# Two chunks' first products drawn forward, two sums of x moved to accumulating DMAs, and another order of the first loads, in a gated FNet and SwiGLU kernel

## The chip, the cores and the metric

The kernel runs on one core of one Trainium2 chip. The metric is the device time of one execution in microseconds. Three runs of the kernel before took 710.97, 711.2 and 711.49 us; their median is 711.2.

## The reference

Two branches work on the same x of 2048 tokens by 512 features. Branch A is a Fourier mixing: the real part of a discrete Fourier transform over features and tokens, written as matrix products. Branch B is a SwiGLU feed-forward network with 1376 hidden units. A sigmoid of a weighted sum over x mixes the two.

```python
def reference(A_x, A_dft_seq_re, A_dft_seq_im, A_dft_hid_re, A_dft_hid_im,
              B_x, B_w1, B_w3, B_w2, gate_w):
    x = A_x
    g = _sigmoid((x * gate_w).sum(-1, keepdims=True))
    # branch A
    a_ = x @ dft_hid_re.T ; b_ = x @ dft_hid_im.T
    a = dft_seq_re @ a_ - dft_seq_im @ b_
    # branch B
    b = (_silu(x @ w1) * (x @ w3)) @ w2
    return g * a + (1 - g) * b
```

The lines between are shortened here to the products they make; x is in float32, as are all operands.

## The kernel before

**Precision.** Each float32 operand is split in two: a high half, which ScalarE writes by copying to float32r (`high`, L108), and a low half, which VectorE writes by subtracting the high half from the operand (`low`, L111). `mm3` (L117) then makes one product out of three matmuls of 128x128 by 128x512: high by high, high by low, low by high, all summed in one PSUM bank.

**The gate and up products.** The hidden units are taken in chunks of 128. For one chunk, w1 and w3 together with the two halves of the features make four blocks A11, A12 (w1) and A21, A22 (w3), each stored as 128x256; they lie in this order beside one another, except that A22 comes before A21, in the input `w13`, and `load_w` brings a chunk (or columns `lo` to `hi` of its four blocks) to a tile `ws`. x is cut likewise into B11, B12, B21, B22 for each of two groups of 1024 tokens; `load_xo` brings one block, 128x1024 or 512 KB, to a tile `xs`. A chunk and a group make an item. Most items use a scheme of seven block products instead of eight (`gate_up`). It needs sums of the blocks: of x the sums T1 = B12 - B11, T2 = B22 - T1, T3 = B22 - B12 and T4 = B21 - T2 (`SUMS`, made by `sum_xo` on VectorE, L207), each split again (`split_xo`) into the tile `xo`; of the weights four sums (`sums_wb`, L248 to L251) that go to a tile `wb`. The blocks A11, A12 and A22 are split to a tile `wa` by `prep_wa`.

**Item 0** is done plainly, with eight block products (`plain`), because no sums exist yet at the start. It is a generator: the code asks for its next piece with `next(step)` after it has prepared the operands of that piece. Its four results are C00, C10, C01 and C11. In the order of the pieces: A11 B11 into C00; A21 B11 into C10; then A12 B21 and A22 B21 complete them; then the same with B12 and B22 for C01 and C11.

**Items 1, 2, 3 ...** begin with `first1` (A11 B11 into a bank X, evicted by ScalarE to the tile s1, L285), `first2` (A12 B21 into a bank Y, added to s1 by VectorE, L293) and `gate1` (Silu of s1 on ScalarE). `gate_up(n)` then makes five further products: into X with T2, T1 (further on with B22), into Z with T3 and T4, and calls `first1` and `first2` of item n + 3 between them. The first Z product of item 1 reads T3 and the second reads T4.

**Order.** Up to the loop over `gate_up`, the instructions of each engine are put in order by the framework's scheduler, by its own costs, from the code's order and the data they need. From `manual_schedule` on they stand as written. Each engine works through its instructions in that order and waits at each for what it needs. The SP queue issues loads, the POOL queue issues stores of h (`store_h`, to `hsp`) and of wb (to `wbsp`). Before the first operands are there, TensorE runs 11 matmuls on a zero tile (L398).

**Buffers.** The four raw x blocks live in four 128x1024 places (`F4`); T2 overwrites B11's place, T3 B12's and T4 B21's, and T1 has a place of its own. The second group's blocks take the same four places, so their loads wait until the splits of T2, T3 and T4 are done. Chunk w shares its place with chunk w + 4.

**After this.** The rest of the kernel is the down projection and the Fourier products (L119 as P in the profile), which the change does not touch.

Of the kernel before, what the change touches and what calls it, by code (L numbers as in the profile page):

```python
# [9 lines left out]
AF = mybir.ActivationFunctionType  # L10
ALU = mybir.AluOpType
# [21 lines left out]
def fnet_swiglu_gate_kernel(  # L33
# [20 lines left out]
    nc = tc.nc  # L54
# [25 lines left out]
    def bank(k, name):  # L80
        return psum.tile([P, 512], F32, tag=f"ps{k}", name=name)
# [14 lines left out]
    def wide(name):  # L96
        return take(F4, [P, 1024], F32, name)
# [9 lines left out]
    def high(hi, src):  # L107
        nc.scalar.activation(hi, src, AF.Copy)  # L108

    def low(hi, lo, src):  # L110
        nc.vector.tensor_sub(lo, src, hi.bitcast(F32))  # L111

    def split(hi, lo, src):
        high(hi, src)
        low(hi, lo, src)

    def mm3(ps, ah, al, bh, bl, first, last, chain=False):  # L117
        for n, (u, v) in enumerate(((ah, bh), (ah, bl), (al, bh))):
            nc.tensor.matmul(ps, u, v, start=first and n == 0, stop=last and n == 2,  # L119
                             skip_group_check=chain)  # L120

# [67 lines left out]
    XO, ST = {}, {}  # L189
    XRAW = ("B12", "B11", "B21", "B22")  # L190
# [4 lines left out]
    def load_xo(g, k):  # L195

        if g not in XO:
            XO[g] = (xo1 if g else xo0).tile([P, 2, 7, 2, 512], F32R, tag="xo", name=f"xo{g}")
        ST[g, k] = wide(f"xs{g}_{k}")
        nc.sync.dma_start(ST[g, k], xt[g, XRAW.index(k)])  # L200

    OPS = ("B11", "B21", "B22", "T1", "T2", "T3", "T4")
    SUMS = {"T1": ("B12", "B11"), "T2": ("B22", "T1"), "T3": ("B22", "B12"), "T4": ("B21", "T2")}

    def sum_xo(g, k, t):
        ST[g, k] = t
        nc.vector.tensor_sub(t, *(ST[g, v] for v in SUMS[k]))  # L207

    def xo_parts(g, k):
        o = XO[g][:, :, OPS.index(k)]  # L210
        return flat_x(o[:, 0]), flat_x(o[:, 1]), ST[g, k]

    def split_xo(g, k):
        split(*xo_parts(g, k))
# [6 lines left out]
    def load_w(w, lo=0, hi=4):  # L221
        if lo == 0:
            WS[w] = f4_a.tile([P, 4, 256], F32, tag=f"f4_{4 + w % (LOOK + 1)}", name=f"ws{w}")
        nc.sync.dma_start(WS[w][:, lo:hi].rearrange("p a n -> p (a n)"),  # L224
                          w13[SETS[w], :, lo * 256 : hi * 256])
# [7 lines left out]
    def wa_parts(w, lo, hi):  # L233
        return (*(flat(WA[w][:, h, lo:hi]) for h in range(2)), flat(WS[w][:, lo:hi]))

    def prep_wa(w, lo=0, hi=3):

        if lo == 0:
            WA[w] = wap.tile([P, 2, 3, 256], F32R, tag="wa", name=f"wa{w}")
        split(*wa_parts(w, lo, hi))  # L240
# [24 lines left out]
    def prep_wb(w):  # L265
        sums_wb(w)
        high_wb(w)
        low_wb(w)

    def prod(ps, n, wi, xi, start, chain=False):  # L270
        w = WSET[n]
        w, wi = (WA[w], wi) if wi < 3 else (WB[w], wi - 3)
        x = XO[ITEMS[n][1]]
        for q in range(2):
            sl = slice(q * P, (q + 1) * P)
            mm3(ps, w[:, 0, wi, sl], w[:, 1, wi, sl], x[:, 0, xi, q, :], x[:, 1, xi, q, :],
                start and q == 0, q == 1, chain)
# [3 lines left out]
    def first1(n):  # L281
        x = bank(n % 4, f"X{n}")
        prod(x, n, 0, 0, True)
        s1 = s1p.tile([P, 512], F32, tag="s1", name=f"s1_{n}")
        nc.scalar.activation(s1, x, AF.Copy)  # L285
        G[n] = (x, s1)

    def first2(n):

        y = bank(4 + n % 2, f"Y{n}")  # L290
        prod(y, n, 1, 1, True)
        s1 = G[n][1]
        nc.vector.tensor_add(s1, s1, y)  # L293
        put_score(n, 0, s1)

    def gate1(n):
        nc.scalar.activation(G[n][1], G[n][1], AF.Silu)
# [19 lines left out]
    def store_h(n, k, h):  # L317

        c, g = ITEMS[n]
        j = min(c % (NP2 - 1) if c < NC - 1 else NP2 - 1, NP2 - 1)  # L320
        b = 2 * (NP2 - 1 <= c < NC - 1)
        nc.gpsimd.dma_start(hsp[g, b + k, j // 2, :, j % 2 * 512 : (j % 2 + 1) * 512], h)  # L322
# [5 lines left out]
    def run(work, n):  # L328
        for f in work.get(n, ()):
            f()  # L330

    def gate_up(n):
# [56 lines left out]
        store_h(n, 1, g1)  # L389
        run(at_end, n)  # L390

    load_w(0, 0, 1)
    load_xo(0, "B11")
    warm = s1p.tile([P, 1024], mybir.dt.bfloat16, tag="s1", name="warm")[:, :512]
    nc.vector.memset(warm, 0.0)
    wps = bank(7, "wps")
# [4 lines left out]
    def plain(b12, a21):  # L401

        c = {}

        def half(i, j, w, x, start):
            if start:
                c[i, j] = bank((0, 4, 6, 7)[2 * i + j], f"C{i}{j}")
            for r in range(2):
                sl = slice(r * P, (r + 1) * P)
                mm3(c[i, j], w(0, sl), w(1, sl), x(r, 0), x(r, 1), start and r == 0,  # L410
                    not start and r == 1)

        def wa(k):
            return lambda h, sl: WA[0][:, h, k, sl]

        def xb(k):
            return lambda q, h: XO[0][:, h, k, q, :]

        w21 = lambda h, sl: a21[:, h, sl]
        x12 = lambda q, h: b12[:, h, q * 512 : (q + 1) * 512]  # L420
        s1 = s1p.tile([P, 512], F32, tag="s1", name="s1_0")
        g1 = u4p.tile([P, 512], F32, tag="u4", name="g1_0")
        h = hp.tile([P, 1024], F32, tag="h", name="h0")
        yield half(0, 0, wa(0), xb(0), True)
        yield half(1, 0, w21, xb(0), True)
        half(0, 0, wa(1), xb(1), False)
        nc.scalar.activation(s1, c[0, 0], AF.Silu)
        yield half(1, 0, wa(2), xb(1), False)
        nc.vector.tensor_mul(h[:, :512], s1, c[1, 0])
        store_h(0, 0, h[:, :512])  # L430
        half(0, 1, wa(0), x12, True)
        yield half(1, 1, w21, x12, True)
        half(0, 1, wa(1), xb(2), False)
        nc.scalar.activation(g1, c[0, 1], AF.Silu)
        half(1, 1, wa(2), xb(2), False)
        nc.vector.tensor_mul(h[:, 512:], g1, c[1, 1])
        yield store_h(0, 1, h[:, 512:])

    load_w(0, 1, 4)
    load_xo(0, "B21")  # L440
    load_xo(0, "B12")
    load_w(1)
    load_xo(0, "B22")
    load_w(2)
    load_w(3)

    zt = parts("b12"), parts("a21")
# [3 lines left out]
    for q in range(2):  # L451
        split(XO[0][:, 0, 0, q], XO[0][:, 1, 0, q], ST[0, "B11"][:, q * 512 : (q + 1) * 512])
    next(step)
    split(a21[:, 0], a21[:, 1], WS[0][:, 3])
    next(step)
    prep_wa(0, 1, 3)
    split_xo(0, "B21")
    next(step)
# [4 lines left out]
    free(*zt)  # L463
    WS.pop(0)
    load_w(4)
    prep_wa(1)
    first1(1)
    first2(1)
    gate1(1)
    sum_xo(0, "T1", hp.tile([P, 1024], F32, tag="h", name="t1"))  # L470
    sum_xo(0, "T2", ST[0, "B11"])
    prep_wa(2)
    first1(2)
    first2(2)
    gate1(2)
    split_xo(0, "T2")
    prep_wb(1)
    sum_xo(0, "T3", ST[0, "B12"])
    split_xo(0, "T3")
    prep_wa(3)  # L480
    first1(3)
# [1 line left out]
    gate1(3)  # L483
    split_xo(0, "T1")
    prep_wa(4)
    sum_xo(0, "T4", ST[0, "B21"])
    split_xo(0, "T4")
    free(*(ST[0, b] for b in ("B11", "B21", "B12", "B22")))

# [84 lines left out]
    n = NI - 1 - LOOK  # L574
# [248 lines left out]
    def step(m):  # L823
# [19 lines left out]
        for r in range(2):  # L843
            sl = slice(r * P, (r + 1) * P)
            for n, zn in steps:
                for i in range(ni):
                    w = ws[2 * n + i]
                    b = slice(i * 512, (i + 1) * 512)
                    mm3(ps[r], w[:, 0, f, sl], w[:, 1, f, sl], zn[:, 0, b], zn[:, 1, b],
                        own and n == 0 and i == 0, n == NQ[blk] - 1 and i == ni - 1, not own)  # L850
# [57 lines left out]
    for i, (src, sp, p) in enumerate(late):  # L908
        blk, b = 1 + i // 2, i % 2
        n = (17, 24)[b]  # L910
# [84 lines left out]
```

## Time and profile before

| | us |
|---|---|
| median of three runs | 711.2 |
| the profiled execution, its own time | 710.88 |
| the span of its trace | 709.1 |
| TensorE busy | 703.9 |
| VectorE busy | 604.6 |
| ScalarE busy | 369.6 |

The profile was taken in one execution. Its time of 710.88 us contains the span of 709.1 us, from the first to the last recorded instruction, and what lies around it. The granted TensorE clock is full through the span. Times within the trace are counted from the span's start. In a row of the timeline stand the start, the duration, the engine, the line of the kernel, the operation with its tiles (out<-in), the shapes and the number of instructions merged in the row; in brackets stands how long the engine was idle before it and what released it. PE is TensorE's matmul, PEld its weight load, DVE VectorE, ACT ScalarE, POOL GpSimd, SPq the queue of SyncE. Numbers behind tile names are left out, so `xo` stands for any operand of x, `wa` for any chunk's split blocks.

### The profile page before, as it was taken

How to read it: one execution, taken by the hardware profiler on the slowest of the kernel's cores; microseconds unless marked ns; L12 is line 12 of the kernel's file. 1: busy time of each engine (PE TensorE's matmuls, PEld its weight loads, DVE VectorE, ACT ScalarE, POOL GpSimd, SP SyncE). 2: the span in 40 equal slices, each digit the busy share in tenths (PEclk: the TensorE clock that was granted, in tenths of full speed). 3: DMA queues.
4: the chain of work that ended last, by engine and by line, in shares of the span. 5: the costliest groups of instructions: out<-in, count | busy, mean ns of one | idle time of the engine just before them, and what ended most of it. 6: DMA issues, size and time to landing. Idle time of an engine off the chain costs nothing.

```text
span 709.1 us, 8589 instructions
## 1 busy us (share of the span) xinstructions
PE 703.9 (99%) x3089; PEld 579.1 (82%) x3089; DVE 604.6 (85%) x733; ACT 369.6 (52%) x478; POOL 64.0 (9%) x118
## 2 busy tenths in 40 slices
PE   9999999999999999999999999999999999999997
PEld 6888888888888888888888888888888888888886
DVE  6979988787679999887999599969997896898985
ACT  6665555655446754454554553544455455455451
POOL 0011111121110000000110001100110000000000
PEclk9999999999999999999999999999999999999999
DMA  7575546589997556712596238814999971773932
GB/s 281 196 295 215 211 188 253 186 313 359 413 412 271 220 207 232 288 60 89 175 358 254 90 122 322 342 48 190 382 419 416 354 270 58 296 285 135 323 119 89
DMA packets 45403, 172.54 MB, mean 243 GB/s; under 512 B 5296, under 2 KB 5424, under 8 KB 41520
## 3 DMA queue, kind: packets, MB, share of 16 engines
q1 hardware_dynamic: 32464, 118.50, 45.2%
q0 software_dynamic: 12608, 52.97, 18.9%
q8 instruction: 24, 0.39, 0.2%
q10 hardware_dynamic: 288, 0.52, 0.2%
q14 instruction: 19, 0.16, 0.1%
HBM read 114.82 MB, written 57.16 MB: 243 GB/s over the span
## 4 chain that ended last, share of the span: by engine, by line
PE 99%; DMA 1%; DVE 0%; ACT 0%; SPq 0%; issue 0%
PE P L119 69%; PE X L119 16%; PE Z L119 8%; PE Y L119 4%; PE C L119 2%; DMA xs_B<-xt 1%; DVE xo L111 0%; DVE zc L788 0%; ACT xo L108 0%; SPq L224 0%
## 5 line engine op out<-in xcount | busy, mean ns | idle before, releaser
L119 PE MATMUL P<-zo,a 128*128 128x512 f32 x1344 | 305.5, 390 | 0.0
L119 PEld LDWEIGHTS P<-zo,a 128*128 128x128 f32 x1344 | 252.1, 188 | 53.2 <-DVE zo L111 1.2
L108 ACT ACTIVATE zo<-B 128x1024 fp32r<-128x1024 f32 (+1 forms) x182 | 189.3, 1045 | 184.5 <-PE P L119 93.2
L111 DVE TENSOR_TENSOR zo<-B,zo 128x1024 fp32r<-128x1024 f32 (+1 forms) x182 | 217.9, 1204 | 48.2 <-ACT zo L108 47.4
L119 PE MATMUL P<-zo,H 128*128 128x512 f32 x468 | 106.2, 389 | 0.0
L119 PEld LDWEIGHTS P<-zo,H 128*128 128x128 f32 x468 | 87.9, 188 | 18.2
L645 DVE TENSOR_TENSOR B<-B,B 128x1024 f32<-128x1024 f32 (+1 forms) x78 | 93.0, 1192 | 0.1
L119 PE MATMUL X<-xo,wb 128*128 128x512 f32 x378 | 92.7, 390 | 0.0
L119 PEld LDWEIGHTS X<-xo,wb 128*128 128x128 f32 x378 | 71.0, 188 | 14.7
L119 PE MATMUL P<-zo,Y 128*128 128x512 f32 x336 | 76.3, 390 | 0.0
L119 PEld LDWEIGHTS P<-zo,Y 128*128 128x128 f32 x336 | 63.1, 188 | 13.1
L322 POOL DMA_DIRECT2D hsp<-h x42 | 23.0, 547 | 126.5 <-DVE h L373 75.6
L119 PE MATMUL X<-xo,wa 128*128 128x512 f32 x126 | 32.3, 390 | 0.0
L119 PE MATMUL Z<-xo,wa 128*128 128x512 f32 x126 | 32.3, 391 | 0.0
L119 PE MATMUL Y<-xo,wa 128*128 128x512 f32 x126 | 32.1, 390 | 0.0
L119 PE MATMUL Z<-xo,wb 128*128 128x512 f32 x126 | 32.1, 390 | 0.0
L648 DVE TENSOR_TENSOR B<-B,B 128x1024 f32<-128x1024 f32 x26 | 31.7, 1219 | 0.0
L863 ACT ACTIVATE zu<-P 128x512 f32<-128x512 f32 x32 | 19.1, 598 | 20.4 <-PE P L119 20.3
L367 DVE TENSOR_TENSOR u<-u,X 128x512 f32<-128x512 f32 x21 | 14.4, 687 | 17.7 <-PE X L119 15.5
L119 PEld LDWEIGHTS Z<-xo,wa 128*128 128x128 f32 x126 | 23.6, 188 | 5.3 <-DVE xo L111 0.4
L119 PEld LDWEIGHTS Y<-xo,wa 128*128 128x128 f32 x126 | 23.7, 188 | 4.9
L119 PEld LDWEIGHTS X<-xo,wa 128*128 128x128 f32 x126 | 23.7, 188 | 4.9
(134 smaller groups left out, 551.3 us busy)
## 6 DMA issues: line engine op xcount, KB each, us to landing
B<-cc SPq DMA_DIRECT2D x64, 512.0 KB, 6.1
hsp<-h POOLq DMA_DIRECT2D x42, 256.0 KB, 3.6
B<-hsp SPq DMA_DIRECT2D x20, 512.0 KB, 9.9
wbsp<-wb POOLq DMA_DIRECT2D x8, 1024.0 KB, 4.3
wb<-wbsp SPq DMA_DIRECT2D x8, 1024.0 KB, 7.8
B<-zsp SPq DMA_DIRECT2D x16, 512.0 KB, 8.4
H<-w2sp SPq DMA_DIRECT2D x6, 1024.0 KB, 9.0
ws<-w SPq DMA_DIRECT2D x11, 512.0 KB, 6.1
```

Source lines behind the costliest of these rows:

```text
L108: nc.scalar.activation(hi, src, AF.Copy)
L111: nc.vector.tensor_sub(lo, src, hi.bitcast(F32))
L119: nc.tensor.matmul(ps, u, v, start=first and n == 0, stop=last and n == 2, skip_group_check=chain)
L322: nc.gpsimd.dma_start(hsp[g, b + k, j // 2, :, j % 2 * 512 : (j % 2 + 1) * 512], h)
L367: nc.vector.tensor_add(u4, u4, x)
L645: nc.vector.tensor_add(t, t, RAW[blk, b, q][:, :n])
L648: nc.vector.tensor_sub(t, RAW[blk, "B12", q], t)
L863: nc.scalar.activation(U[name][:, r], ps[r], AF.Copy)
```

## The change

1. The first load issued is now B11 of x, then A11 of chunk 0. A11 of chunk 1 and of chunk 2 (128x256 each) are loaded by themselves, ahead of the rest of their chunk; A11 of chunk 1 also comes ahead of the rest of chunk 0.
2. A11 of chunks 1 and 2 are split by themselves, and `first1(1)` and `first1(2)` are called between the pieces of item 0: after A11 B11 of item 0 and after A21 B11. In the code `first2` and `gate1` of both items stay where they were.
3. In C00's products the three terms come in another order: high by high, low weights by high x, high weights by low x (`low_last`).
4. T3 and T4 are no longer made by VectorE. `minus_xo` negates the subtrahend (B12, then T2) in its own place on ScalarE and then issues, on the POOL queue, a DMA that adds the first operand (B22, then B21) from the input `xt` in device memory onto the negated tile. T4 lies therefore in the place of T2, which was B11's. T1 and T2 are sums on VectorE as before.

```diff
-    def mm3(ps, ah, al, bh, bl, first, last, chain=False):
-        for n, (u, v) in enumerate(((ah, bh), (ah, bl), (al, bh))):
+    def mm3(ps, ah, al, bh, bl, first, last, chain=False, low_last=False):
+        terms = ((ah, bh), (al, bh), (ah, bl)) if low_last else ((ah, bh), (ah, bl), (al, bh))
+        for n, (u, v) in enumerate(terms):
...
+    def minus_xo(g, k, t):
+        b, c = SUMS[k]
+        ST[g, k] = t
+        nc.scalar.activation(t, t, AF.Copy, scale=-1.0)
+        nc.gpsimd.dma_start(t, xt[g, XRAW.index(b)], accum_op=ALU.add)
...
+    load_xo(0, "B11")
     load_w(0, 0, 1)
-    load_xo(0, "B11")
...
                 mm3(c[i, j], w(0, sl), w(1, sl), x(r, 0), x(r, 1), start and r == 0,
-                    not start and r == 1)
+                    not start and r == 1, low_last=i == j == 0)
...
+    load_w(1, 0, 1)
     load_w(0, 1, 4)
+    load_w(2, 0, 1)
     load_xo(0, "B21")
     load_xo(0, "B12")
-    load_w(1)
+    load_w(1, 1, 4)
     load_xo(0, "B22")
-    load_w(2)
+    load_w(2, 1, 4)
     load_w(3)
...
     next(step)
+    prep_wa(1, 0, 1)
+    first1(1)
     split(a21[:, 0], a21[:, 1], WS[0][:, 3])
     next(step)
+    prep_wa(2, 0, 1)
+    first1(2)
     prep_wa(0, 1, 3)
     split_xo(0, "B21")
...
-    prep_wa(1)
-    first1(1)
+    prep_wa(1, 1, 3)
     first2(1)
     gate1(1)
     sum_xo(0, "T1", hp.tile([P, 1024], F32, tag="h", name="t1"))
     sum_xo(0, "T2", ST[0, "B11"])
-    prep_wa(2)
-    first1(2)
+    prep_wa(2, 1, 3)
     first2(2)
     gate1(2)
+    minus_xo(0, "T3", ST[0, "B12"])
     split_xo(0, "T2")
     prep_wb(1)
-    sum_xo(0, "T3", ST[0, "B12"])
+    minus_xo(0, "T4", ST[0, "T2"])
     split_xo(0, "T3")
...
     prep_wa(4)
-    sum_xo(0, "T4", ST[0, "B21"])
     split_xo(0, "T4")
```

## The prediction

> **What bounds the kernel now.** I read the page first: the busy shares and the chain that ended last.
>
> ```profile
> span 709.1 us, 8589 instructions
> ...
> PE 703.9 (99%) x3089; PEld 579.1 (82%) x3089; DVE 604.6 (85%) x733; ACT 369.6 (52%) x478; POOL 64.0 (9%) x118
> ...
> PE 99%; DMA 1%; DVE 0%; ACT 0%; SPq 0%; issue 0%
> ```
>
> TensorE sets the time almost alone: 99% of the span and of the chain. The change leaves the number of matmuls as it is, so it can only win time in which TensorE waits, and any new wait of TensorE lengthens the kernel one to one. The timeline of the first 20 us and of 19 to 45 us shows where it waits.
>
> ```profile
> 0.74 0.39 SPq L224 DMA_DIRECT2D ws<-w  x1
> 1.19 0.42 SPq L200 DMA_DIRECT2D xs_B<-xt  x1
> ...
> 3.21 0.42 ACT L108 ACTIVATE wa<-ws 128x256 fp32r<-128x256 f32 x1 [0.96 <-DMA ws<-w]
> ...
> 4.94 1.15 ACT L108 ACTIVATE xo<-xs_B 128x512 fp32r<-128x512 f32 x2 [1.31 <-DMA xs_B<-xt]
> ...
> 5.60 1.29 DVE L111 TENSOR_TENSOR xo<-xs_B,xo 128x512 fp32r<-128x512 f32 x2 [1.51 <-ACT xo L108]
> ...
> 5.62 0.50 PE L119 MATMUL C<-xo,wa 128*128 128x512 f32 x1
> ...
> 6.35 1.43 PE L119 MATMUL C<-xo,wa 128*128 128x512 f32 x5 [0.22 <-DVE xo L111]
> ...
> 7.19 1.06 ACT L108 ACTIVATE xo<-xs_B 128x1024 fp32r<-128x1024 f32 x1 [0.27 <-DMA xs_B<-xt]
> ...
> 8.46 1.06 ACT L108 ACTIVATE b<-xs_B 128x1024 fp32r<-128x1024 f32 x1 [0.21 <-DMA xs_B<-xt]
> ...
> 8.98 3.15 PE L119 MATMUL C<-xo,wa 128*128 128x512 f32 x12
> ...
> 9.57 2.14 PEld L119 LDWEIGHTS C<-xo,wa 128*128 128x128 f32 x10 [0.40 <-DVE xo L111]
> 9.74 0.84 ACT L108 ACTIVATE wa<-ws 128x768 fp32r<-128x768 f32 x1 [0.22 <-DMA ws<-w]
> ```
>
> ```profile
> 20.29 1.36 PE X L119 x6
> ```
>
> ```profile
> 31.00 1.83 PE L119 MATMUL Z<-xo,wa 128*128 128x512 f32 x6
> ...
> 31.40 0.99 PEld L119 LDWEIGHTS Z<-xo,wa 128*128 128x128 f32 x5 [0.43 <-DVE xo L111]
> ```
>
> Six matmuls take 1.36 us on the chain (0.227 each), and a recorded group of n ends 0.39 us after its last start. So twelve should show 11 x 0.227 + 0.39 = 2.89 us; the group at 8.98 shows 3.15, a wait of about 0.25. Six should show 1.53; the group at 31.00 shows 1.83, a wait of 0.30. The third wait is the second matmul: the first stands at 5.62, the next at 6.35. Together with that half microsecond some 1.05 us can be won, 0.15% of the time. After that no wait of note stands in the chain.
>
> The same rows show what the waits hang on: all three end with VectorE's low half of a split of x. VectorE is full there:
>
> ```profile
> 15.00:20.00 5.00, 5.00 (x24) 4.15 (x23) 5.00 (x9) 3.89 (x7) 0.41 (x1) 1.00 0.04 14
> 20.00:25.00 5.00, 5.00 (x24) 4.15 (x23) 5.00 (x6) 3.53 (x5) 0.68 (x2) 1.00 0.66 234
> 25.00:30.00 5.00, 5.00 (x24) 4.14 (x23) 4.92 (x7) 2.88 (x6) 0.00 (x0) 1.00 0.40 156
> ```
>
> In these windows by 5 us the third busy column is VectorE: 5.00, 5.00 and 4.92 of 5. So whatever leaves VectorE or comes to it before 31 us counts.
>
> **How I walk through the changed program.** I take each engine's instructions in the changed program's order and start each when its engine is free and its inputs are there, with these durations and overlaps:
>
> ```profile
> L111 DVE TENSOR_TENSOR xo<-xs_B,xo 128x1024 fp32r<-128x1024 f32 x7 | 8.6, 1222 | 0.6 <-ACT xo L108 0.6
> L111 DVE TENSOR_TENSOR wa<-ws,wa 128x768 fp32r<-128x768 f32 x7 | 6.7, 952 | 0.0
> L108 ACT ACTIVATE xo<-xs_B 128x1024 fp32r<-128x1024 f32 x7 | 7.4, 1058 | 0.8 <-DVE xs_B L207 0.5 <-DMA xs_B<-xt 0.3
> L285 ACT ACTIVATE s<-X 128x512 f32<-128x512 f32 x7 | 4.2, 594 | 3.6 <-PE X L119 3.6
> L293 DVE TENSOR_TENSOR s<-s,Y 128x512 f32<-128x512 f32 x6 | 4.1, 680 | 0.0
> L250 DVE TENSOR_TENSOR wu<-ws 128x256 f32<-128x256 f32 x5 | 2.1, 419 | 0.0
> ```
>
> ```profile
> 21.60 1.22 DVE L111 TENSOR_TENSOR wb<-wu,wb 128x1024 fp32r<-128x1024 f32 x1
> ...
> 22.74 1.22 DVE L111 TENSOR_TENSOR xo<-xs_B,xo 128x1024 fp32r<-128x1024 f32 x1
> ```
>
> Back to back, two VectorE instructions of 1.22 start 1.14 apart, so 0.08 of each is overlap; ScalarE overlaps by 0.10 (two halves of 0.62 take 1.15 above). From the end of VectorE's low half to the matmul it releases there are 0.05 (5.60 + 0.69 = 6.29, matmul at 6.35); where TensorE had been idle, the weight load is no longer hidden, another 0.11.
>
> **Part 1, the first x block first.** The queue moves 512 KB in 1.27 us (the seen landings 7.19, 8.46, 9.74). B11 was seen at 4.94, with 128 KB ahead of it. If the issue time decides it lands 0.45 earlier (1.19 - 0.74), at 4.49; if the bytes decide, 128 KB or 0.32 earlier, at 4.62. I take 4.54, between them. ScalarE's first half then ends at 5.16, VectorE's low half runs 5.19 to 5.88. But wa's high half now comes after B11 (its bytes land by 4.94, ScalarE 5.06 to 5.47), and its low half after that of B11: 5.80 to 6.21. The new order of the three terms asks for exactly this one at the second matmul. It stands at 6.26 instead of 6.35 (6.37 with its weight load): -0.09, with the two landings -0.14 and -0.01.
>
> **Part 2, A11 B11 of chunks 1 and 2 in between.** Twelve matmuls move forward, 2.72 us of cover before B21 is needed. B21 now lands behind 1,792 KB instead of 1,536 KB: 7.19 + 0.64 = 7.8. ScalarE does not take it then, because the eviction of X1 stands ahead of it and waits for X1's last matmul (6.37 + 10 x 0.227 + 0.39 = 9.03): eviction to 9.67, B21's high half to 10.63, VectorE's low half 10.66 to 11.88. The matmul that reads it is the 27th, at 6.37 + 25 x 0.227 = 12.05. Just in time: the 0.25 at 8.98 goes, -0.25. The split of wa into two pieces for two chunks costs VectorE two more instructions, two issues more on SP (0.45 each, ahead of B21) that the full queue covers. B12, B22 and the rests of the two chunks land at most 0.64 later than before, and ScalarE comes to each of them over a microsecond after that.
>
> **Part 3, VectorE's chain after it.** VectorE idles from 8.4 to 10.66 and is then busy without a gap worth counting up to the low half of T3. In the changed order that stretch holds nine of 128x1024, one of 128x768, six of 128x512 and four of 128x256: 9 x 1.22 + 0.95 + 6 x 0.685 + 4 x 0.42 = 17.7, less 19 overlaps of 0.084 is 16.1, plus about 0.3 of short waits: it ends at 27.07. T1's low half stands ahead of T3's in this order, which it did not before. The matmul that reads T3's low half is the 92nd, due at 6.37 + 90 x 0.227 = 26.80; it can start at 27.07 + 0.16 = 27.23. A new wait: +0.43. I leave 0.2 on either side for the short waits.
>
> **Part 4, T3 and T4 by accumulating DMA.** Two VectorE sums of 1.22 go; two negations on ScalarE (1.06 each by the 128x1024 row) and two 512 KB DMAs on POOL come. For T4: VectorE ends T2's low half at 22.39, ScalarE negates 22.75 to 23.81, POOL issues at 24.12 (0.31 after its releaser, the first two rows below). T4's low half is wanted by the 110th matmul, 27.23 + 18 x 0.227 = 31.31. Back from it: low half ended by 31.15, begun by 29.9, high half begun by 28.8. So the DMA may take 4.7 us. T3's, issued at 19.02, may take 5.7, for ScalarE is at T3 only at 24.75, after the Silu of chunk 2.
>
> ```profile
> 12.24 0.69 DVE L429 TENSOR_TENSOR h<-s,C 128x512 f32<-128x512 f32 x1 [0.25 <-PE C L119]
> ...
> 13.25 0.69 POOL L322 DMA_DIRECT2D hsp<-h  x1 [12.80 <-DVE h L429]
> ```
>
> ```profile
> hsp<-h POOLq DMA_DIRECT2D x42, 256.0 KB, 3.6
> ...
> wbsp<-wb POOLq DMA_DIRECT2D x8, 1024.0 KB, 4.3
> ```
>
> ```profile
> DMA to landing us min/median/max: 5.0/5.0/5.0
> ```
>
> ```profile
> DMA to landing us min/median/max: 8.6/8.6/8.6
> ```
>
> ```profile
> 28.63 4.03 SPq L200 DMA_DIRECT2D xs_B<-xt  x4
> ...
> 32.76 6.83 SPq L224 DMA_DIRECT2D ws<-w  x2
> ```
>
> No accumulating DMA stands in the trace. From POOL, 256 KB take 3.6 us from issue to landing and 1024 KB 4.3 in the median. The two rows after that are single stores of 1024 KB: the one issued at 23.1, almost alone on the queues, with 5.0, and the one at 34.7, beside the loads in the last rows, with 8.6. An accumulate reads 512 KB from memory and 512 KB from the tile, so it lies nearest the 1024 KB rows. I take 4.5, between 4.3 and 5.0: T4 lands at 28.6 and TensorE doesn't wait. The bounds are 3.6 and 8.6. With T4 in time, the 0.30 that stood at 31.00 goes: -0.30; at 5.0 it would stay. SP's loads of the second x half, at 28.63 before, now wait for T4's split (about 30.9), and the chunk load behind them leaves at 32.8 as before, so nothing follows there. On POOL's queue T4 stands behind the second store of h, which its multiply frees at 21.1, and ahead of the store of wb at 25.0, which nobody reads soon.
>
> The Trainium skill, Collectives: The Full Stack, section "The bandwidth ceiling: the fold count and why AG ≠ RS ≠ AR", says that a DMA that adds has two sources to read on one ring and so gets half of the copy's rate. By that rule, an estimate: 2 x 1.27 = 2.54 us of transfer where a copy has 1.27; the sum stays as it is so long as the rest of the DMA stays under 2.1 us. No trace here shows an accumulate yet.
>
> **Sum.** -0.09 - 0.25 + 0.43 - 0.30 = -0.21 us. The profiled execution took 710.88 with its span of 709.1, so 710.7 for it. The median of the runs is 711.2, 0.3 above: 711.0.
>
> **Rivals.**
> 1. The accumulate is late, and the kernel is slower. Place: T4's high half on ScalarE, and everything queued behind it there (Silu of chunk 3, evictions of Z1 and X4). From 4.7 us on, each microsecond of the DMA is one of TensorE's. At 8.6: 711.0 + 3.9 = 714.9. For it: the 8.6, the 5.0 of the store that stood in the same place, and that nothing here shows what an addition costs. Against it: the 8.6 came beside six loads, and in 24 to 29 us the changed program has none under way. It exceeds 0.2% (1.42 us, about what a measurement of this kernel can tell from no change) from about 6.3 us.
> 2. A little late, 4.7 to 6.3 us: 711.0 to 712.6, about 711.8 at 5.5.
> 3. T3's wait is not there, because VectorE has slack in it that I have not seen: -0.64, 710.6. Against it: the sum of part 3 is of durations that scatter by a few ns.
> 4. The change moves but doesn't win: small loads of 128 KB hold B11's followers up, the landing is byte-bound (-0.01), and B21's low half, just in time by 0.01, comes 0.1 late: -0.03, 711.2.
>
> **Chances.** Forecast 0.40, with its own range 710.6 to 711.4; rival 1 0.38 (an operation without a price, and the smallest margin of the walk hangs on it); rival 2 0.11; rival 3 0.05; rival 4 0.06. Above 0.2% stands rival 1: slower 0.38. Faster by 1.42 us is more than all the waits together; it keeps 0.03 out of rival 3 for something unseen. The rest, 0.59, is within 0.2%. The range leaves out 0.03 below 710.4 and, of rival 1, what lies over 715.0.
>
> **What would show it.** The second matmul at 6.26; no idle before the 25th to 30th matmul (the first group of A12 B21); a wait of about 0.43 at the first Z, released by VectorE's xo; issue to landing of the two accumulates near 4.5, and no wait at T4's product near 31.3. Wrong if the accumulates take over 4.7, which shows as TensorE waiting for ScalarE or VectorE at the Z group that reads wa, or if TensorE waits before 20 us.

## The result and the profile after

| | before | after |
|---|---|---|
| median of six runs, us | 711.27 (710.97 to 712.11) | 715.58 (713.59 to 715.71) |
| ratio, with its 95% interval | | 1.0055 (1.0045 to 1.0066) |
| the profiled execution, us | 710.88 | 715.66 |

The changed kernel is slower by 4.3 us. Its page begins with these rows: the span, the busy times, and the chain that ended last.

```profile
span 713.9 us, 8604 instructions
...
PE 706.0 (99%) x3089; PEld 579.9 (81%) x3089; DVE 602.9 (84%) x733; ACT 371.3 (52%) x482; POOL 65.9 (9%) x120
...
PE 97%; DMA 1%; DVE 1%; ACT 1%; issue 0%; ACTq 0%
```

TensorE's share of the chain is 97%, where it was 99%. Its busy time has grown too, by 2.1 us, with the same 3089 matmuls: some of them took longer. Both are found in one place. In the windows of the kernel after, the columns are the window, its length, the busy time of TensorE, its weight loads, VectorE, ScalarE and GpSimd (number of instructions in brackets), the granted clock, the DMA share and GB/s.

```profile
20.00:25.00 5.00, 5.00 (x24) 4.14 (x23) 4.96 (x8) 5.00 (x8) 1.48 (x3) 1.00 0.78 165
25.00:30.00 5.00, 2.54 (x10) 1.52 (x9) 2.40 (x4) 2.17 (x4) 0.82 (x2) 1.00 0.98 228
30.00:34.00 4.00, 3.92 (x10) 3.14 (x11) 3.15 (x6) 2.06 (x3) 0.00 (x0) 0.57 0.57 233
```

Between 25 and 30 us TensorE, VectorE and ScalarE are each busy for about half the time, and the DMA engines are full (0.98). In the window after that the granted clock is 0.57: ten matmuls took four microseconds. A matmul that should start 0.227 us after the one before it starts there 0.427 us after it, and the trace has the clock at half from 29.99 to 33.41 us. The chain that ended last, in order of time, says what TensorE waited for (start, length, what):

```profile
19.41 8.27 DMA xs_B<-xt
27.69 0.02 issue
27.71 1.07 ACT xo L108
28.78 0.02 issue
28.80 1.24 DVE xo L111
30.04 0.04 issue
30.08 2.50 PE Z L120 x5
32.58 3.21 PE X L120 x12
```

It is T3's accumulating DMA, issued at 19.41 and landed at 27.69, then T3's high half, then its low half. The timeline of the same stretch adds the transfers beside it:

```profile
19.41 0.91 POOL L216 DMA_DIRECT2D xs_B<-xt  x1 [2.73 <-ACT xs_B L215]
...
20.09 0.33 SPq L233 DMA_DIRECT2D ws<-w  x1
...
24.40 0.86 POOL L216 DMA_DIRECT2D xs_B<-xt  x1 [2.08 <-ACT xs_B L215]
...
28.82 0.50 PE L120 MATMUL Z<-xo,wb 128*128 128x512 f32 x1 [1.78 <-ACT xo L108]
...
30.08 2.50 PE L120 MATMUL Z<-xo,wb 128*128 128x512 f32 x5 [0.76 <-DVE xo L111]
...
31.22 1.06 ACT L108 ACTIVATE xo<-xs_B 128x1024 fp32r<-128x1024 f32 x1 [1.48 <-DMA xs_B<-xt]
```

At 20.09 SP issues the load of chunk 5, 0.7 us behind T3's DMA. T4's DMA lands at 31.2, when TensorE runs again at the half clock, and nothing on TensorE waits for it. The view of the two accumulates has the times from issue to landing, T4's 6.8 and T3's 8.3:

```profile
L216 POOL DMA_DIRECT2D xs_B<-xt x2: 863/884/906, 19.4 to 24.4; - x2
...
DMA to landing us min/median/max: 6.8/7.5/8.3
```

The 8.3 us have two parts. In the trace's records fifteen of the 16 DMA engines had finished T3's DMA by 26.54, 7.1 us after its issue, and chunk 5's load by 26.72; the last engine finished them only at 27.69 and 27.84. Between 19 and 29 us the list of DMA queues has, beside the transfers of the kernel, a single packet of 16 KB of the kind `instruction`:

```profile
q8 instruction: 1, 0.02, 0.6%
```

It runs from 25.54 to 26.50. It may be the reason for the last 1.15 us. That is not shown: the records don't name the engine of a packet, no run tests it by itself, and the load of B21 has a last engine 1.2 us behind the others (8.64 and 9.84) without such a packet.

What the starts of neighbouring matmuls show over their 0.227 us adds up to the loss. At the first two Z matmuls: 1.95 and 1.03 of waiting. Behind them, 0.11 for a weight load that a wait leaves unhidden, and 1.54 over eight matmuls for the half clock. Of the old waits, the second and third matmul keep 0.35 of 0.61 but the first one starts 0.19 later, the 0.25 at the product with B21 stays in this execution, and the 0.28 at T4 is gone. So 1.95 + 1.03 + 0.11 + 1.54 + 0.35 + 0.19 - 0.61 - 0.28 = 4.28; the last matmul of the kernel starts 4.36 later than before.

### The profile page after: what moved, and what is told of

It is laid out like the page before. It is cut to its first block, busy times and chain, and to the rows that moved or that the text cites. A ratio compares the mean times of both kernels' runs of the same rounds, so it can differ in the third digit from the quotient of the medians.

```text
span 713.9 us, 8604 instructions
## 1 busy us (share of the span) xinstructions
PE 706.0 (99%) x3089; PEld 579.9 (81%) x3089; DVE 602.9 (84%) x733; ACT 371.3 (52%) x482; POOL 65.9 (9%) x120
## 3 DMA queue, kind: packets, MB, share of 16 engines
q0 software_dynamic: 12896, 54.02, 19.6%
## 4 chain that ended last, share of the span: by engine, by line
PE 97%; DMA 1%; DVE 1%; ACT 1%; issue 0%; ACTq 0%
PE P L120 68%; PE X L120 16%; PE Z L120 8%; PE Y L120 3%; DMA xs_B<-xt 1%; PE wps L407 1%; PE C L120 1%; DVE xo L111 0%; ACT xo L108 0%; DVE t L208 0%; ACT xs_B L215 0%; DVE zc L801 0%; ACT s L436 0%; ACT wa L108 0%; DVE warm L404 0%
## 5 line engine op out<-in xcount | busy, mean ns | idle before, releaser
L120 PEld LDWEIGHTS Z<-xo,wb 128*128 128x128 f32 x126 | 24.2, 193 | 8.2 <-ACT xo L108 2.2
```

## The experiments

Each kernel is measured against the kernel before on the same chip, which took 711.32 us (median of 26) beside the accumulate alone, the moved load, the filled stall and parts 1 to 3; 711.43 (27) beside the two kernels with plain copies, part 1 alone and parts 1 and 4 together; and 711.52 (9) beside the two with GpSimd. The theory: T3's accumulate comes too late because an accumulate is slow by itself and slower beside chunk 5's load; the stall then halves the clock. The rivals: parts 1 to 3 make the loss, or any DMA in this place would.

### The DMA without its addition

```diff
-        nc.gpsimd.dma_start(t, xt[g, XRAW.index(b)], accum_op=ALU.add)
+        nc.gpsimd.dma_start(t, xt[g, XRAW.index(b)])
```

The changed kernel, with the operand copied over the negated tile instead of added to it: the sums T3 and T4 are left out.

> The changed kernel with plain copies of B22 and B21 in the place of the two accumulating DMAs; the additions are left out, so T3 and T4 are not the sums. Theory (adding doubles what each packet takes, and that on top of the shared load makes 8.3 us): packets take about 165 ns instead of 327, T3's copy lands 5 to 6 us after its issue, no half clock, 711.3 to 712.3. Rival (the company on the queues alone is at fault): T3's copy still takes over 7.5 and the time stays at 715.

Measured: 711.05 us, ratio 0.9994 (0.9985 to 1.0003). The two copies:

```profile
L216 POOL DMA_DIRECT2D xs_B<-xt x2: 539/548/556, 19.1 to 24.1; - x2
...
DMA to landing us min/median/max: 3.7/3.8/4.0
```

Without the addition the loss is gone, with the same instructions and the same bytes from memory in the same places. The company on the queues alone is thus not at fault; the theory, though, expected 5 to 6 us for T3's copy, and it took 3.7. The chain of this kernel in the same stretch now runs through VectorE:

```profile
23.67 1.14 DVE wb L111
24.80 2.30 DVE xo L111 x2
27.10 0.04 issue
27.15 1.45 PE Z L120 x5
```

That is part 3 of the prediction with its own numbers: VectorE ends T3's low half at 27.10 (27.07 forecast), and the second Z product starts at 27.15 (27.23 forecast), 0.35 us late. No other wait is left after 7 us.

### The accumulate alone, in the kernel before

```diff
+    minus_xo(0, "T3", ST[0, "B12"])
     split_xo(0, "T2")
     prep_wb(1)
-    sum_xo(0, "T3", ST[0, "B12"])
+    minus_xo(0, "T4", ST[0, "T2"])
...
-    sum_xo(0, "T4", ST[0, "B21"])
```

> The kernel before with only the two accumulating DMAs. By the walk T3's is issued near 15.5, when the queues are quiet, and T4's near 21.9. Theory (an accumulate alone takes about 5, and it was the company on the queues that made 8.3 and 6.8): T3 lands by 20.6 and waits for nothing; T4 in 4.5 to 5.4 gives 711.0 to 711.3, at 6.5 it gives 712.1. Rival (adding costs 7 to 8 us whatever else is on the queues): T4 at 8.3 gives +2.6, 713.9.

Measured: 711.20 us, ratio 1.0002 (0.9993 to 1.0012).

```profile
L215 POOL DMA_DIRECT2D xs_B<-xt x2: 863/884/906, 15.9 to 22.2; - x2
...
DMA to landing us min/median/max: 5.4/5.4/5.5
```

Here T3's DMA leaves at 15.9, 3.5 us earlier than in the changed kernel, and lands at 21.4, when chunk 5's load, issued at 19.5, has moved a fifth of its bytes. It takes 5.5 us, T4's 5.4, and TensorE waits for neither. So an accumulate of 512 KB costs about 5.4 us nearly without company, not 8.3; and part 4 alone neither wins nor loses in the median. Six of its ten runs took 710.72 to 711.28 us and four 712.14 to 712.90. The trace is of one of the six; what the four waited for is not known.

To price the addition, the same kernel was run with plain copies (again without the sums T3 and T4; one run).

> The kernel before with only part 4, with plain copies instead of accumulates (the additions are left out). It measures the price of the addition alone, on quiet queues: the accumulates took 5.5 and 5.4 there. Theory (half the rate while bytes move, the rest as in a copy): 128 rows over 16 engines at 327 less 165 ns are 1.3 us less, so 4.1 and 4.1. Rival (the addition has a fixed cost of its own, in issue and completion): near 3.4. The time stays near 711.2 in both.

Measured: 711.17 us.

```profile
L215 POOL DMA_DIRECT2D xs_B<-xt x2: 542/550/558, 16.1 to 22.4; - x2
...
DMA to landing us min/median/max: 3.6/4.0/4.5
```

T3's copy takes 3.6 where its accumulate took 5.5: the addition costs 1.9 us there. T4's takes 4.5 instead of 5.4, so only 0.9 less. In the trace's records one packet of 4 KB takes 327 ns with the addition and 159 to 173 without. Each of the 16 DMA engines carries eight of them, so 8 x 0.16 = 1.3 us of the 1.9 is the transfer. More than half of the rest is its start: the first packet runs 1.6 us after the issue instead of 1.26, and the issuing instruction itself takes 0.9 us instead of 0.55.

### Chunk 5's load put behind T3's accumulate

```diff
-        nc.sync.dma_start(WS[w][:, lo:hi].rearrange("p a n -> p (a n)"),
+        (nc.gpsimd if w == 5 else nc.sync).dma_start(WS[w][:, lo:hi].rearrange("p a n -> p (a n)"),
```

The changed kernel; the load is issued on POOL's queue, behind T3's DMA, instead of beside it from SP.

> The changed kernel with the load of chunk 5 on the POOL queue, behind T3's accumulate, instead of beside it on SP's. Theory (sharing the DMA engines with this 512 KB load made T3's 8.3 us): T3 lands 5 to 5.5 us after its issue, the wait of 1.9 at the first Z goes, and with it the half clock; T4, now behind the load, lands near 29.5 and costs up to 1: 711.5 to 712.5. Rival (the addition itself is that slow): T3 stays near 8 us and the time at 715.6.

Measured: 712.59 us, ratio 1.0018 (1.0009 to 1.0028).

```profile
L216 POOL DMA_DIRECT2D xs_B<-xt x2: 872/894/917, 19.1 to 24.1; - x2
...
DMA to landing us min/median/max: 5.3/5.9/6.6
```

T3 falls from 8.3 to 5.3 us: without the load beside it, it comes in time. It lands at 24.34 here, before the packet of the kind `instruction`, so this run doesn't part that packet's share from the load's. The wait at the first Z matmuls shrinks from 3.09 (1.95 + 1.03 + 0.11) to the 0.35 of part 3. Now T4, behind the moved load, takes 6.6, and the wait appears at its place:

```profile
PE Z L120 <- ACT u L368: 1.5, 1, 1.5
```

The starts of the matmuls give 1.84 us for it, and the clock stays full. The table gathers the times from issue to landing:

| kernel | T3's | T4's | chunk 5's load |
|---|---|---|---|
| after | 8.3 | 6.8 | 7.8, beside T3's |
| chunk 5's load behind T3's | 5.3 | 6.6 | 7.7, between the two |
| after, without the additions | 3.7 | 4.0 | 4.9 |
| before with part 4 alone | 5.5 | 5.4 | 3.9, after T3's |
| the same without the additions | 3.6 | 4.5 | 3.9 |

### The stall filled with idle matmuls

```diff
         prod(x, n, 4, 4, False, True)
+        if n == 1:
+            fill = bank(6, "fill")
+            for _ in range(2):
+                prod(fill, 1, 0, 0, True)
```

The changed kernel with twelve further matmuls, whose result nobody reads, just ahead of the first Z product.

> The changed kernel with twelve matmuls more (2.72 us) ahead of the first Z product of item 1, where TensorE waited 1.9 and 1.0 us; their result is not used. Theory (the half clock of 3.4 us that follows is set by these gaps): the gaps hold the twelve for nothing and the clock stays full, 8 matmuls at 427 instead of 227 ns go: 1.6 us less, 714.0. Rival (the clock drop has another cause, or the waits simply move): 715.6, and if the twelve are not hidden up to 717.

Measured: 713.83 us, ratio 1.0033 (1.0019 to 1.0047). More work, and 1.75 us less than the changed kernel. Its windows:

```profile
25.00:30.00 5.00, 4.72 (x22) 3.60 (x21) 2.14 (x3) 2.03 (x3) 0.39 (x1) 1.00 1.03 251
30.00:34.00 4.00, 4.00 (x18) 3.30 (x18) 2.95 (x5) 2.55 (x4) 0.00 (x0) 1.00 0.47 193
```

The clock is 1.00 in both, and 18 matmuls start in the second window where ten did. The wait for T3 itself isn't shortened by this; so the half clock costs about as much as the starts of the matmuls say (1.54). One of the six runs of the changed kernel, the one of 713.59, has a mean granted clock of 0.999 where the others have 0.997, and is 2.0 us shorter: it fits a run without the halving, but it was not traced.

### Parts 1 to 3 alone

```diff
-    minus_xo(0, "T3", ST[0, "B12"])
     split_xo(0, "T2")
     prep_wb(1)
-    minus_xo(0, "T4", ST[0, "T2"])
+    sum_xo(0, "T3", ST[0, "B12"])
...
+    sum_xo(0, "T4", ST[0, "B21"])
```

The changed kernel with both sums back on VectorE.

> The changed kernel with T3 and T4 as VectorE sums again, so parts 1 to 3 alone. Theory (the late accumulates make the whole loss, and the halved clock behind them belongs to it): near the kernel before, 710.7 to 711.7. Rival (the early products and small loads lose by themselves, since VectorE idles until B21 is split and has 1.22 us twice more to do after it): the walk with the landings of the changed kernel gives waits of 1.06 at wb's low half and 0.6 at T4, together +1.6: 712.8.

Measured: 712.56 us, ratio 1.0018 (1.0008 to 1.0027). The waits of TensorE:

```profile
PE X L120 <- DVE wb L111: 0.8, 1, 0.8
PE Z L120 <- DVE xo L111: 0.3, 1, 0.3
```

By the starts of the matmuls these are 1.04 us at the first product with `wb` and 0.59 at T4's. Parts 1 to 3 alone lose 1.2 us; the rival was right here. Two windows say why, first of the kernel before, then of this one:

```profile
5.00:10.00 5.00, 4.78 (x19) 3.09 (x18) 3.90 (x6) 4.30 (x7) 0.00 (x0) 1.00 1.02 415
10.00:15.00 5.00, 5.00 (x24) 4.13 (x23) 4.75 (x6) 3.77 (x5) 0.69 (x1) 1.00 0.92 368
...
5.00:10.00 5.00, 5.00 (x18) 3.48 (x17) 3.45 (x7) 3.30 (x8) 0.00 (x0) 1.00 0.95 368
10.00:15.00 5.00, 5.00 (x23) 4.06 (x22) 3.89 (x6) 4.51 (x7) 0.00 (x0) 1.00 1.03 415
```

VectorE is busy for 3.45 + 3.89 = 7.34 of these ten microseconds; in the kernel before it was 3.90 + 4.75 = 8.65. While TensorE runs the matmuls drawn forward, VectorE waits for the high half of B21, and the 1.3 us are missing later, when it is full. Part 4, which takes two sums of 1.22 from it, pays that back (711.05 with the fast DMAs).

### Part 1 alone

```diff
-    load_w(0, 0, 1)
     load_xo(0, "B11")
+    load_w(0, 0, 1)
```

The kernel before, with this and with the other order of the three terms in C00.

> The kernel before with only part 1: B11's load first, then A11 of chunk 0, and the other order of the three terms in C00; no early products, no small loads of chunks 1 and 2, no accumulates. Theory (part 1 was right, and it is the small loads that brought B21 from 7.2 to 9.8): second matmul 0.1 earlier, B21 landed by 7.8, 711.0 to 711.3. Rival (B11 first holds the later loads up by itself): B21 past 9 and a wait of 1 to 2 us at the 25th... here the 13th matmul: 712.5 to 713.

Measured: 712.05 us, ratio 1.0009 (1.0000 to 1.0018), a loss if any. The timeline:

```profile
4.48 0.63 ACT L108 ACTIVATE xo<-xs_B 128x512 fp32r<-128x512 f32 x1 [2.23 <-DMA xs_B<-xt]
...
5.67 0.42 ACT L108 ACTIVATE wa<-ws 128x256 fp32r<-128x256 f32 x1 [0.56 <-DMA ws<-w]
...
6.14 1.91 PE L120 MATMUL C<-xo,wa 128*128 128x512 f32 x6 [0.74 <-ACT wa L108]
...
8.10 1.06 ACT L108 ACTIVATE xo<-xs_B 128x1024 fp32r<-128x1024 f32 x1 [0.54 <-DMA xs_B<-xt]
```

B11 is there at 4.48 (4.94 before), but A11, a quarter of its bytes, lands 1.2 us after it, and the first matmul starts at 6.14 instead of 5.62. B21 follows at 8.10 instead of 7.19, though the same bytes stand ahead of it. What B11 wins is lost by what now stands behind it. Part 1 and part 4 together in the kernel before gave no more.

> A version meant to keep what paid: parts 1 and 4 without the early products, so that T3's accumulate is issued near 15.3 with the queues quiet and T4's near 22. Theory: second matmul 0.1 earlier, no wait at T4 (0.3 before), perhaps 0.2 at T1: the walk gives -0.25, 711.0, which the spread of the runs can hardly tell from the kernel before. Rival (T4's accumulate, with the load of chunk 5 before it, is late as in the changed kernel): over 712.

Measured: 711.93 us, ratio 1.0009 (1.0000 to 1.0018).

### The two sums on GpSimd

A DMA is not the only way to take the sums from VectorE. Both kernels were run with them as subtractions on GpSimd, both called ahead of T2's split:

```diff
-        nc.vector.tensor_sub(t, *(ST[g, v] for v in SUMS[k]))
+        eng = nc.gpsimd if g == 0 and k in ("T3", "T4") else nc.vector
+        eng.tensor_sub(t, *(ST[g, v] for v in SUMS[k]))
```

The changed kernel so:

> The changed kernel with T3 and T4 as subtractions that GpSimd computes itself, from the blocks already on the chip: no negation, no DMA. Theory (all that was wrong was the price of the accumulate): like the run with plain copies, 711.0 to 711.5, with 0.2 to 0.4 of waiting at T3's low half. Rival (VectorE and GpSimd at work at once slow each other, or GpSimd needs over 3.5 us for 128x1024): VectorE's 1.22 grows in that stretch, over 712.

Measured: 713.77 us, ratio 1.0034 (1.0021 to 1.0048). The kernel before so:

> The kernel before with only that: T3 and T4 by GpSimd, no early products, no other loads. Theory: the 0.3 at T4 goes and nothing comes, 711.0 (the walk gives -0.2 up to 2.5 us a subtraction, and nothing at 3.5). Rival (as above): VectorE slowed, 711.5 to 712.5.

Measured: 714.77 us, ratio 1.0049 (1.0035 to 1.0062). Both lose. Rows of the second, from its timeline:

```profile
14.52 3.25 POOL L208 TENSOR_TENSOR xs_B<-xs_B,xs_B 128x1024 f32<-128x1024 f32 x1 [0.26 <-DVE t L208]
...
15.44 3.43 DVE L208 TENSOR_TENSOR xs_B<-xs_B,t 128x1024 f32<-128x1024 f32 x1
...
22.40 3.52 DVE L111 TENSOR_TENSOR wa<-ws,wa 128x768 fp32r<-128x768 f32 x1
22.71 2.38 POOL L208 TENSOR_TENSOR xs_B<-xs_B,xs_B 128x1024 f32<-128x1024 f32 x1
```

VectorE's sum of 1.22 us takes 3.43 and its low half of 0.95 takes 3.52, each while a subtraction runs on GpSimd: the work taken from VectorE is paid with a longer wait on it. No kernel tried here beats the kernel before by more than a measurement can tell.

## Why the prediction was wrong

The forecast was 711.0, with 710.4 to 715.0 around it; the result is 715.58, on the side to which the forecast gave 0.38.

**Part 1 (forecast -0.09).** The second matmul stands at 6.27 in the profiled run, as forecast (6.26). Its inputs came otherwise: B11 earlier, A11 later. The timeline of the kernel after:

```profile
4.09 0.63 ACT L108 ACTIVATE xo<-xs_B 128x512 fp32r<-128x512 f32 x1 [1.84 <-DMA xs_B<-xt]
...
5.34 0.42 ACT L108 ACTIVATE wa<-ws 128x256 fp32r<-128x256 f32 x1 [0.62 <-DMA ws<-w]
...
5.81 1.90 PE L120 MATMUL C<-xo,wa 128*128 128x512 f32 x6
...
9.86 1.06 ACT L108 ACTIVATE xo<-xs_B 128x1024 fp32r<-128x1024 f32 x1
10.96 1.23 DVE L111 TENSOR_TENSOR xo<-xs_B,xo 128x1024 fp32r<-128x1024 f32 x1 [1.52 <-ACT xo L108]
```

B11 was seen at 4.09, not 4.54, and A11 at 5.34, not 5.06. The two errors cancel, so that the 6.26 came true by luck. In five other traced executions with the same first loads B11 is seen at 4.25 to 4.60, A11 at 5.15 to 5.34, and the second matmul stands at 6.08 to 6.35: executions differ by more than the gain that was forecast. The run with part 1 alone shows that the step by itself wins nothing.

**Part 2 (forecast -0.25).** The wait stayed in the profiled execution, but not in most others. B21 landed at 9.84 (issued at 3.07, 6.8 from issue to landing), not at 7.8 as its bytes gave. The forecast had ScalarE busy until 9.67 anyway, so a delay of 2 us cost only the 0.14 in which ScalarE then waited, and the overlap of 0.10 that an instruction behind a wait doesn't have; but the margin at TensorE was 0.12. ScalarE began at 9.86, VectorE ended at 12.18 instead of 11.88, and the wait stayed. Five other traced kernels begin with the same loads and products. B21 landed in them at 9.02 to 9.59; in four the wait was gone and in one, with the sums on GpSimd, 0.16 was left. So the cover was enough, as forecast, though only just; the landing by bytes was wrong in all six. Rival 4 had named this margin.

**Part 3 (forecast +0.43).** Right, a little large. Where the accumulates don't hide it, the wait is there, at the place named and 0.35 long, in two kernels (without the additions, and with chunk 5's load moved).

**Part 4 (forecast: 4.5 us for an accumulate, T3 with 5.7 to spare and T4 with 4.7; -0.30).** This is the step that failed. The value of 4.5 was chosen between 4.3 and 5.0 as the nearest rows. Alone the operation takes 5.4 to 5.5; it would have cost T4 about 0.7. T3's took 8.3, 2.6 over what it had to spare, beside the load of chunk 5, issued 0.7 us after it; with that load behind it, it took 5.3. Had the last engine kept up with the other fifteen, it would have been 7.1, still 1.4 over (an estimate from the trace). The forecast looked for loads in 24 to 29 us, where T4's DMA runs, and found none there (by then chunk 5's should have landed; it was under way until 27.84). It did not look at 19 to 24, where T3's runs. Nor was the load unknown. In the timeline of the kernel before it stands at 20.02:

```profile
20.02 0.33 SPq L224 DMA_DIRECT2D ws<-w  x1
```

The bounds, up to 8.6, did hold both values; what was missing was the second place at which the upper bound decides, T3's. The tolerances themselves were right to 0.2: T3's 8.27 is 2.57 over its 5.7, and the wait over part 3's 0.35 is 2.74. T4's 6.56 in the kernel with chunk 5's load moved is 1.86 over its 4.7, and the wait is 1.84. In the changed kernel T4's delay of 6.8 costs nothing more, since T3's stall moved its due time back.

**What no step priced.** The half clock after the stall, 1.54 us in the trace; the run with idle matmuls, where it is absent, is 1.75 shorter. Without it the result would have stood at about 714 (an estimate), inside the range.

**The rivals.** Rival 1 was right in mechanism (an accumulate that comes late, from a certain point on one to one), wrong in place (T4, where T3 comes first), and its 714.9 rests on the bound of 8.6 at T4, not on this course of things. Rival 2's 5.5 us is what an accumulate takes nearly without company. Rival 3 fell: part 3's wait is there.

**The sum.** With the accumulate's price taken out, the rest of the sum agrees with the trace: without the additions the last matmul starts 0.20 us earlier than in the kernel before, and the forecast was -0.21. The measured time there, 711.05 against 711.43 on that chip, can't be told from no change. In the traces the last matmul of the changed kernel starts 4.56 us later than without the additions: 2.74 of T3's wait, 1.54 of clock and 0.25 at B21, which is scatter of the executions, make 4.53.

**The rate of the addition.** The Trainium skill, Collectives: The Full Stack, section "The bandwidth ceiling: the fold count and why AG ≠ RS ≠ AR", has the adding step of a ring between ranks at half the rate of the copying one, because it reads two sources; the prediction carried this over to a DMA from memory onto a tile. The packets agree (327 ns against 159 to 173). The estimate from it allowed 2.1 us for the rest of the DMA and counted on the sum as long as that held; the rest was about 2.9 (5.5 - 2.6) in a quiet queue, so the rate was right, and the sum didn't stay as it was.

## What to carry to other kernels

A transfer whose price no row shows has to be put at its upper bound at every place where it is used, with the tolerance of each place and the list of all transfers that run in that stretch; here two rows of the timeline of before (the load at 20.0, the store at 19.6) would have shown the company that T3's DMA gets. A stall of TensorE of some 3 us is priced with what follows it, 1.5 us of half clock here. A wait of a few tenths in a single trace is compared with other executions of the same start before it is called an effect: here B21's landing alone moved by 0.8 us between them. And an edit that moves a full engine's work forward is measured by what that engine does afterwards, not by the wait that it removes at the start.

## What the hardware showed that was not expected

- **The clock.** It fell to half for 3.41 us after two waits of 1.8 and 0.8 us of idle time with one matmul between them, so not after one long gap. A wait of 1.84 us in the kernel with chunk 5's load moved did not bring it down. The Trainium skill, TensorE: Matmul & The Clock Gate, section "What's actually happening", has a free-running window of 3413 ns and a half clock after an idle window. The length agrees; the window ahead of the fall, 26.58 to 29.99 us by that length, was not idle throughout, for TensorE was busy in it until 27.03, and a matmul of 0.50 us stands behind that; idle it was for 2.46 of the 3.41 us. A wait of 2.19 us in the kernel before with GpSimd's sums left the clock full in its trace, too. Two of that kernel's five runs, and one of 27 of the kernel before, have a mean clock of 0.997 like the runs with the halving, but none of them was traced; so what decides is not shown.
- **Sharing among DMAs.** T3's accumulate and a load of the same 512 KB took 8.3 and 7.8 us side by side; 5.5 and 3.9 one after the other. Both were complete only at the end (27.69 and 27.84), but fifteen of the 16 engines were done 1.1 us earlier in each. In the run with the filled stall it is the same: T3's DMA was complete by 26.41 on fifteen engines and at 27.42 on the last, with a packet of the kind `instruction` from 25.24 to 26.17. How the queues divide the engines is not shown.
- **The order of the first loads.** B21's landing moved from 7.17 to 9.84 us, by 2.67, where 0.64 was due by the bytes. In the changed kernel the first of the 16 DMA engines ended B21 at 7.74 and the last at 9.84; before, 6.65 and 7.17. Over the traced executions it landed at 7.17 to 7.69 with the loads of the kernel before (four executions), at 8.08 and 8.41 with part 1, which puts no further bytes ahead of it (two), and at 9.02 to 9.84 with part 1 and the small loads of chunks 1 and 2 (six). So part of the delay comes with B11 ahead of A11, and the small loads add 0.6 to 1.8 us to it. Why the order matters is not shown.
- **VectorE beside GpSimd.** The Trainium skill, SBUF — State Buffer, section "Who interferes with whom", has a VectorE instruction with two SBUF inputs in contention with a GpSimd instruction that reads SBUF. The trace agrees: 1.22 us became 3.43. It isn't always VectorE that is slowed: in the changed kernel with GpSimd's sums, T3's subtraction took 5.07 us on GpSimd, while a sum and a low half that lie wholly within it kept their 1.22 and 0.95 on VectorE; the next low half, begun in its last part, took 2.83.
